# The middle heads' q of batch 0: its load goes from SyncE's queue to ScalarE's, behind an activation-table load

## The chip, the cores and the metric

The kernel runs on one core of a Trainium2 chip. The metric is the device time of one execution in microseconds (us), lower is better. Besides the unprofiled runs there is one profiled execution, from which all rows shown here come. Times inside an execution count from the start of its span.

## The reference

Eight batches of twelve heads of attention, each head 448 positions of 64 values, feed a two-layer network with a tanh GELU. All inputs and the output are float32.

```python
def rmsnorm(x, g):
    rms = np.sqrt(np.mean(x * x, axis=-1, keepdims=True) + 1e-06)
    return x / rms * g
q_n, k_n = (rmsnorm(q, g_q), rmsnorm(k, g_k))      # q, k, v: (8, 12, 448, 64)
scores = q_n @ k_n^T / sqrt(64)
attn = softmax(scores) @ v
x = attn with the heads side by side               # (3584, 768)
out = gelu_tanh(x @ w_in) @ w_out                  # w_in (768, 2048), w_out (2048, 768)
```

## The kernel before, in words

Heads are handled in groups of four. A batch `b` has three groups, `c` = 0, 1, 2, and for each group and each of q and k there is one tile, `raw`, of 128 partitions by 896 float32 (448 KB, two pairs of heads). The "middle heads" of batch 0 are the group `c` = 1. In the profile every such tile is called rawq or rawk, whatever its batch and group.

A tile goes through these steps before it can be used: it is squared (`square`, line 159 on ScalarE or line 161 on GpSimd), the squares are summed per row on VectorE (`total`, line 170), ScalarE turns the sums into reciprocal roots with a logarithm and an exponential (`rsqrt`, lines 195 to 214), and the tile is multiplied by them (`normed`, line 273). Then TensorE transposes it (`turn`, line 291) and VectorE or ScalarE copies the transposed tile out of PSUM (`put`, lines 300 to 304). `unit(b, c, t)` is one step of attention: TensorE makes a block of scores (line 333) and ScalarE takes its exponential (line 337). One batch has 21 units. After the units of batch 0 the kernel goes over to the network's matrices and the other batches, where TensorE sets the pace.

The order of instructions on each engine is the order in which the program is written (a manual schedule); nothing is moved by a scheduler. A load is a DMA that is issued by the queue of one engine: SyncE's, ScalarE's or GpSimd's. A tile's landing is told by one of eight semaphores that the DMAs of SyncE and ScalarE take in turn, so a DMA may have to wait until the one that had its semaphore before has landed.

At the start, the queues are filled so:

- SyncE's queue: the first half of q of group 0 (line 121), k of group 0 in two parts (line 617), then by `loads(0, 1)` and `loads(0, 2)` the 448 KB tiles q and k of group 1, q and k of group 2 (line 121), then the tiles of batch 1.
- ScalarE's queue: the second half of q of group 0 (line 121), the 64 values of `g_k` (line 86), then the load of the activation table of exponential and logarithm (line 627). Its next instructions are the squares of group 0, which wait for those loads.
- GpSimd's queue: the 64 values of `g_q`, and after some setting up a half of the normalization of group 0's q, then the square of group 1's q, the square of group 1's k in two halves, two loads of v, the squares of group 2, and parts of `w_in`:

```python
    normed(0, 0, "q", nc.gpsimd, t_first)
    ...
    square(0, 1, "q", nc.gpsimd)
    for a in range(2):
        square(0, 1, "k", nc.gpsimd, slice(a, a + 1))
    load_v(0, 0, 2)
```

The roots of group 1 are asked for after the third unit (`(2, lambda: rsqrt(0, 1, near=(0, 1)), ...)`), so ScalarE has three exponentials ahead of them, and all later exponentials behind them. VectorE has the sums of group 1 ahead of the copy of the second part of group 0's transposed k (`put(0, 0, "k", t_rest)`, line 300), which the fifth unit on TensorE needs.

Of the kernel before, what the change touches and what calls it, by code (L numbers as in the profile page):

```python
# [17 lines left out]
def kernel(  # L18
# [11 lines left out]
    nc = tc.nc  # L30
# [84 lines left out]
    def load(b, c, n, parts=1, engs=(nc.sync,)):  # L115
        t = rawqk.tile([P, 2, NT, D], F32, tag=f"raw{n}", name=f"raw{n}")
        src = {"q": q, "k": k}[n]
        raws[n, b, c] = t
        m = 2 // parts
        return [  # L120
            lambda i=i: engs[i].dma_start(
                t[:, i * m:(i + 1) * m].rearrange("p a t d -> p a (t d)"),
                src[b, 4 * c + 2 * i * m:4 * c + 2 * (i + 1) * m].rearrange(
                    "(a r) (p t) d -> (r p) a (t d)", r=2, t=NT
                ),
            )
            for i in range(parts)
        ]

    def loads(b, c):  # L130
        for n in "qk":
            for go in load(b, c, n):
                go()
# [491 lines left out]
        go()  # L625
    load_g(1, g_k, nc.scalar)
    nc.scalar.preload_act_table_set(EXP_SET)
    loads(0, 1)
    loads(0, 2)

    nc.vector.memset(eps, 1e-6)
# [264 lines left out]
```

## Time and profile before

| | |
|---|---|
| median of three runs | 404.31 us (404.3, 404.31, 408.4) |
| time of the profiled execution | 405.4 us |
| its span, first to last instruction | 403.6 us |
| TensorE busy with matmuls | 393.4 us, 97% of the span |
| ScalarE, VectorE, GpSimd busy | 281.0, 257.7, 123.0 us |
| mean granted TensorE clock | 0.999 of full speed |
| moved by DMA | 54.07 MB |

The engines' shares are means over the whole span. The change lies in the first 15 us, where the shares say little; what matters there is which instruction waits for which load, and that is read from the chain of work that ended last, from the waits and from the DMA issues. "SPq", "ACTq" and "POOLq" are the queues of SyncE, ScalarE and GpSimd; among the DMA queues q1 is fed by SyncE, q10 by ScalarE, q0 by GpSimd.

### The profile page before, as it was taken

What the parts mean: (1) busy time and instruction counts of PE and PEld (TensorE: products, weight loads), DVE (VectorE), ACT (ScalarE), POOL (GpSimd) and SP (SyncE); (2) the same over time, 40 slices, a digit from 0 to 9 for tenths busy, and PEclk for the clock granted to TensorE, in tenths of its full rate; (3) what the DMA queues carried; (4) which work ended last, traced back from release to release, by engine and by line L of the source; (5) the groups of instructions that cost most, each with busy time, mean ns of one, the idle gap of its engine ahead of it and who ended that gap; (6) DMA issues with size and microseconds to landing.
All of it is one profiled execution on the core that took longest, in us unless ns stands there. A gap on an engine that the chain in (4) does not pass through costs nothing.

```text
span 403.6 us, 8096 instructions
## 1 busy us (share of the span) xinstructions
PE 393.4 (97%) x3321; PEld 209.8 (52%) x3321; DVE 257.7 (64%) x436; ACT 281.0 (70%) x382; POOL 123.0 (30%) x103
## 2 busy tenths in 40 slices
PE   7799999999999999999999999999999999999996
PEld 3365555555555555554555555555555545555564
DVE  5998858985796369845699357963698405990010
ACT  6995498868974887847975689748878359744301
POOL 4993407364007230093004540072301800000000
PEclk9999999999999999999999999999999999999999
DMA  8999995998515954169612938139413511110033
GB/s 280 312 212 208 200 211 210 239 233 228 97 41 105 256 97 143 41 162 288 107 41 63 255 60 221 40 85 275 69 41 80 115 24 39 50 47 24 2 78 80
DMA packets 65561, 54.07 MB, mean 134 GB/s; under 512 B 37364, under 2 KB 60532, under 8 KB 65524
## 3 DMA queue, kind: packets, MB, share of 16 engines
q1 hardware_dynamic: 53184, 41.48, 38.3%
q0 software_dynamic: 12112, 11.80, 18.8%
q8 instruction: 26, 0.43, 0.4%
q10 hardware_dynamic: 228, 0.28, 0.3%
q14 instruction: 11, 0.09, 0.1%
HBM read 45.61 MB, written 11.01 MB: 140 GB/s over the span
## 4 chain that ended last, share of the span: by engine, by line
PE 94%; ACT 2%; DMA 2%; POOL 1%; DVE 0%; SPq 0%; issue 0%
PE o L443 38%; PE h L422 24%; PE t L473 12%; PE t L333 9%; PE t L384 8%; ACT ex L337 2%; DMA rawq<-in_q_dram 2%; PE o L384 1%; POOL g L161 1%; PE tp L291 1%; SPq L617 0%; PE os L384 0%; DVE st L393 0%; DVE ss L170 0%; PE o L266 0%
## 5 line engine op out<-in xcount | busy, mean ns | idle before, releaser
L337 ACT ACTIVATE ex<-t,shift 128x896 bf16<-128x896 f32 x168 | 157.6, 1005 | 22.0 <-PE t L333 19.4
L443 PE MATMUL o<-wout,g 128*128 128x384 bf16 (+1 forms) x912 | 156.8, 324 | 0.0
L443 PEld LDWEIGHTS <-g 128*128 128x128 bf16 x912 | 83.6, 98 | 67.7 <-issue 18.8
L422 PE MATMUL h<-xT,win 128*128 128x448 bf16 x516 | 99.1, 352 | 0.0
L170 DVE TENSOR_REDUCE ss<-sq 128x14 f32<-128x896 f32 (+3 forms) x45 | 44.3, 999 | 49.1 <-ACT sq L159 46.1
L422 PEld LDWEIGHTS <-win 128*128 128x128 bf16 x516 | 50.5, 98 | 47.1
L428 ACT ACTIVATE g<-h 128x448 bf16<-128x448 f32 x86 | 46.6, 543 | 28.2 <-PE h L422 23.1
L453 DVE COPY osb<-o 128x384 f32<-128x384 f32 x41 | 22.7, 554 | 52.6 <-PE o L443 50.6
L333 PE MATMUL t<-qT,kT 64*64 64x448 bf16 x672 | 47.0, 359 | 3.0 <-DVE kT L300 1.0
L473 PE MATMUL t<-xT,win 128*128 128x448 bf16 x252 | 49.6, 352 | 0.0
L478 ACT ACTIVATE g<-t 128x896 bf16<-128x896 f32 x21 | 18.4, 915 | 33.0 <-PE t L473 33.0
L666 POOL COPY mark<-es 1x1 bf16<-1x1 bf16 x6 | 1.1, 177 | 131.5 <-DVE es L355 131.5
L273 POOL TENSOR_TENSOR nrmq<-rawq,rinv 128x896 bf16<-128x896 f32 (+1 forms) x21 | 34.8, 1658 | 12.0 <-DVE o L236 7.7
L473 PEld LDWEIGHTS <-win 128*128 128x128 bf16 x252 | 24.5, 98 | 22.8 <-issue 0.6
L273 POOL TENSOR_TENSOR nrmk<-rawk,rinv 128x896 bf16<-128x896 f32 x20 | 33.5, 1679 | 0.0
L333 PEld LDWEIGHTS <-kT 64*64 64x64 bf16 x672 | 17.4, 105 | 28.1 <-issue 20.8
L384 PE MATMUL t<-ex,vb 64*64 64x448 bf16 x588 | 31.6, 350 | 0.0
L451 ACT COPY osb<-o 128x384 f32<-128x384 f32 (+1 forms) x16 | 7.3, 458 | 31.5 <-PE o L443 31.5
L400 DVE STREAM_TRANSPOSE rb<-rc 128x896 f32<-128x896 f32 x24 | 26.7, 1111 | 0.8
L358 DVE TENSOR_TENSOR e<-ex 128x896 bf16<-128x896 bf16 x33 | 20.0, 607 | 9.7 <-ACT ex L337 9.4
L384 PEld LDWEIGHTS <-vb 64*64 64x64 bf16 x672 | 20.4, 107 | 11.1 <-issue 2.4
L393 DVE STREAM_TRANSPOSE st<-t 128x448 f32<-128x448 f32 x42 | 24.6, 625 | 1.0 <-PE t L384 0.9
(93 smaller groups left out, 294.5 us busy)
## 6 DMA issues: line engine op xcount, KB each, us to landing
out_dram<-osb SPq DMA_DIRECT2D x54, 192.0 KB, 2.7
rawq<-in_q_dram SPq DMA_DIRECT2D x23, 448.0 KB, 4.3
rawk<-in_k_dram SPq DMA_DIRECT2D x23, 448.0 KB, 5.5
vb<-in_v_dram POOLq DMA_DIRECT2D x7, 672.0 KB, 6.7
win<-in_moe_w_in_dram POOLq DMA_DIRECT2D x8, 384.0 KB, 11.0
wout<-in_moe_w_out_dram POOLq DMA_DIRECT2D x2, 1536.0 KB, 24.0
vb<-in_v_dram POOLq DMA_DIRECT2D x1, 448.0 KB, 10.5
qT<-nrmq SPq DMA_TRANSPOSE x19, 4.9
```

Source lines behind the costliest of these rows:

```text
L170: nc.vector.reduce_sum(sss[b][:, seat(b, c), "qk".index(n), hs, ts], squares(b, c, n, hs, ts), axis=AX.X)
L273: eng.tensor_mul(nrms[n, b, c][:, ts].rearrange("p t a d -> p a t d"), raws[n, b, c][:, :, ts], root[:, :, ts].to_broadcast([P, 2, m, D]),)
L333: nc.tensor.matmul(sc[r * R:(r + 1) * R, a, :S], kT[rs, c, t, r], qT[b][rs, c, :, r], start=True, stop=True,)
L337: nc.scalar.activation(ex[:, t], sc[:, :, :S], AF.Exp, scale=scale, bias=shift)
L384: nc.tensor.matmul(o[r][a * D:(a + 1) * D], vb[b % 2][rs, 2 * c + a, i] if what else ones[rs], es[i][rs, a], start=(i == 0), stop=(i == n ...
L393: nc.vector.transpose(st[:, r].rearrange("p a b -> p (a b)"), oas[0][r])
L400: nc.vector.transpose(rb.rearrange("p r s -> p (r s)"), rc.to_broadcast([128, 2 * S // 32, 32]))
L422: nc.tensor.matmul(h[:, :S], win[:, c, f * 128:(f + 1) * 128], xT[b][:, c], start=(c == 0), stop=(c == HP - 1),)
L428: nc.scalar.activation(g[:, f, (b % 2) * S:(b % 2 + 1) * S], h[:, :S], AF.Gelu_apprx_tanh)
L443: nc.tensor.matmul(o, g[:, f, i * 128:(i + 1) * 128], wout[:, f, lo:hi], start=(f == 0), stop=(f == nf - 1),)
L453: nc.vector.tensor_copy(osb[:, lo:hi], o)
L473: nc.tensor.matmul(h[:, j, :S], win[:, c, f * 128:(f + 1) * 128], xT[b][:, c], start=(c == 0), stop=(c == HP - 1),)
```

## The change

The one load of q of group 1 of batch 0 is issued by ScalarE, behind the table load, and not by SyncE. The loads that stood behind it in SyncE's queue move up by one place. No byte more or less is loaded, no other instruction is added or taken away, and the order of the other engines stays as it was. The semaphores are dealt out a little differently: q of group 1 takes the one that k of group 1 had, and the other way round.

```diff
     load_g(1, g_k, nc.scalar)
     nc.scalar.preload_act_table_set(EXP_SET)
-    loads(0, 1)
+
+    for go in load(0, 1, "q", 1, (nc.scalar,)) + load(0, 1, "k"):
+        go()
     loads(0, 2)
```

`loads(b, c)` issued q and then k of a group, both on SyncE; `load(b, c, n, parts, engs)` gives the issues of one tile, each on the engine named.

## The prediction

> **What bounds the kernel now.** I read the page first, for the engine that sets the end. TensorE is busy for 97% of the span, and it makes up 94% of the chain that ended last. DMA has 2% of that chain, and that is what this change touches.
>
> ```profile
> span 403.6 us, 8096 instructions
> PE 393.4 (97%) x3321; PEld 209.8 (52%) x3321; DVE 257.7 (64%) x436; ACT 281.0 (70%) x382; POOL 123.0 (30%) x103
> PE 94%; ACT 2%; DMA 2%; POOL 1%; DVE 0%; SPq 0%; issue 0%
> ```
>
> Second, the chain in order of time over the first 45 us, to see where those 2% lie. Columns: start, length, what.
>
> ```profile
> 2.20 6.35 DMA rawq<-in_q_dram
> 8.55 0.07 issue
> 8.62 3.47 POOL g L161 x3
> ...
> 12.12 0.63 DVE ss L170
> ...
> 12.77 0.33 ACT lg L195
> ...
> 13.32 0.93 ACT ex L337
> ```
>
> The load of group 1's q, the one that is moved, is itself on the chain: issued at 2.20, landed at 8.55, then GpSimd's three squares of group 1, VectorE's last sum, ScalarE's roots, and from 13.3 the exponentials. So any microsecond by which this landing moves, moves the chain. ScalarE is then full: between 13.25 and the end of its table load at 31.97 its timeline shows one gap, of 0.15 us. TensorE starts the network at 31.50, and the waits after that name nothing that TensorE waits for beyond its own issue. So nothing later absorbs a shift, and a shift of the landing goes to the end one to one.
>
> Third, the timeline of the first microseconds, with the queues. Columns: start, length, engine, line, operation.
>
> ```profile
> 1.19 1.10 ACTq L86 DMA_DIRECT2D grow<-in_g_k_dram  x1
> 2.20 0.47 SPq L121 DMA_DIRECT2D rawq<-in_q_dram  x1
> 2.32 1.28 ACT L627 ACT_TABLE_LOAD   x1 [2.32 <-POOL ident masks.py:197]
> 2.71 0.47 SPq L121 DMA_DIRECT2D rawk<-in_k_dram  x1
> 4.12 1.05 ACT L159 ACTIVATE sq<-rawq 128x448 f32<-128x448 f32 x2 [0.52 <-DMA rawq<-in_q_dram]
> 8.62 1.68 POOL L161 TENSOR_TENSOR g<-rawq 128x896 f32<-128x896 f32 x1 [0.98 <-DMA rawq<-in_q_dram]
> 12.77 0.32 ACT L195 ACTIVATE lg<-ss,eps 128x28 f32<-128x28 f32 x1 [0.77 <-DVE ss L170]
> ```
>
> GpSimd sits idle for 0.98 us for the moved load, and ScalarE for 0.77 us for the roots' sums. These two are all that an earlier landing could win.
>
> **The change part by part.**
>
> *The issue.* On SyncE one issue of 0.47 us goes from 2.20, so k of group 1 is issued at 2.20 in place of 2.71 and q of group 2 at 2.71 in place of 3.23. The next one, k of group 2, stays at 3.91: it waits (0.2 us in SyncE's own waits) until the half tile on ScalarE's queue, which had its semaphore, has landed. The tiles of batch 1 behind it wait in the same way or for buffers, so they stay too. On ScalarE the issue comes after the table load in program order, and it waits for no semaphore. When does it start? The trace shows ScalarE's sequencer running past a table load: at 76.35 a table load starts in the engine, and the sequencer had finished the waits of the two squares behind that load at 76.10 and 76.19. So I take the issue right behind that of `g_k`, at 2.32 or a little later, not at 3.60. It costs 0.37 to 0.47 by the rows of 448 KB, 0.83 by the longest one (SyncE's at 4.33), 1.10 by that of `g_k`. What is queued behind it on ScalarE is the first square, which waits for its own load until 4.12. An issue that ends by 3.4 is hidden by the table load. If it started only after the table load, it would end at 4.07 (0.47, still hidden), 4.43 (0.83) or 4.70 (1.10); the last is 0.58 late for the squares of group 0, and the 0.77 us that ScalarE idles before 12.77 takes it up. The issue itself therefore costs 0.
>
> *The place among the loads.* This is the whole price. The 16 DMA engines are busy from 3 us on (a share of 0.92 to 1.06 in every microsecond), so a tile lands when the bytes ahead of it are done. The issues of the trace, taken one by one, give the landings of the 448 KB tiles on SyncE's queue, in their order: q of group 1 at 8.55 (2.20 + 6.35), k of group 1 at 9.76 (2.71 + 7.05), q of group 2 at 10.95 (3.23 + 7.72), k of group 2 at 12.15 (3.91 + 8.24): 1.2 us a tile. Each line below is the answer for one issue; the last column is the time to landing.
>
> ```profile
> rawq<-in_q_dram SPq DMA_DIRECT2D x1, 448.0 KB, 6.3
> rawk<-in_k_dram SPq DMA_DIRECT2D x1, 448.0 KB, 7.0
> rawq<-in_q_dram SPq DMA_DIRECT2D x1, 448.0 KB, 7.7
> ```
>
> After the change k of group 1 is issued first, and q 0.12 us or more behind it, on another queue. How do the DMA engines serve two queues? The row that answers is at 16.5 to 17.5: a q tile had been issued by SyncE at 14.50 and landed only 7.3 us later, and for this whole microsecond the engines moved packets of GpSimd's queue alone, whose loads of v had been issued from 12.03 on.
>
> ```profile
> q0 software_dynamic: 206, 0.18, 113.1%
> ```
>
> There is no line of q1 in that answer: the later queue waited for most of the earlier one's bytes. Where both queues were issued together (the halves of group 0's q, both at 0.74) they moved together, 24 packets of q1 and 23 of q10 between 2.6 and 2.8. And `g_k`, issued on ScalarE's queue between the two parts of group 0's k, moved at 4.0 to 4.5, amid those parts, though its queue was empty from 3.5. All three rows say: nearly in the order of issue. So q of group 1, issued almost together with k, shares its bytes with k, and both are done when both are done: at 9.76, where k lands now.
>
> The Trainium skill, page "DMA: Bandwidth & Descriptors", section "Queues, rings and completion order", says otherwise: each DMA engine goes round the queues that have work, packet by packet. By it q would have half the rate from its start on, and would land early. The microsecond without q1 does not agree with it, at least not over some 30 packets of an engine; what the sum would be is the first rival.
>
> *The sum.* Landing 9.76 in place of 8.55: +1.21. GpSimd starts the square at 9.83, k has landed by then, so its 3.47 us end at 13.30 in place of 12.09. VectorE, ScalarE's roots and the exponentials follow, each 1.21 later. On VectorE the copy of group 0's k (line 300, at 12.65) stands behind the last sum, so TensorE's fifth unit, now at 13.12, comes later by the same; TensorE's gap there grows from 0.91 to some 2.1 us. Behind GpSimd's squares stand its loads of v and `w_in`; they shift alike, and so do their users. Moved 1.21 us, nothing else: 405.4 + 1.2 = 406.6 us for a profiled execution, whose 405.4 is the span's 403.6 and 1.8 around it. The median of the runs is 1.1 us below the profiled one, so 404.3 + 1.2 = **405.5 us**.
>
> *The bounds.* From below: the landing can be earlier, but the chain wins no more than GpSimd's 0.98 of idle time, and k, the second tile needed, still lands at about 9.76, when both tiles' bytes are done: GpSimd would square its two halves (2 x 0.93) by 11.65, 0.44 earlier. From above: q falls behind q of group 2 (issued at 2.71), landing 10.95, +2.4, or behind k of group 2, 12.15, +3.6; or behind all that SyncE has queued. I take +1.2, because an issue at about 2.35 is nearest to the one at 2.20.
>
> **The rivals.**
>
> *Shared packet by packet from the start (faster).* q's first packets come 1.04 us after the issue, as those of the first half tile on ScalarE's queue did, so at 3.4, and its 16 packets an engine (256 rows of 1,792 bytes over 16 engines) alternate with those of k of group 0. At twice 74 ns, the mean of such a packet in the trace, it is done by about 6, and with the 2 us by which the slowest engines trail (the 16 landings of the tile now spread from 6.26 to 8.55) by 8. For it: the two halves at 2.6. Against it: the second at 16.5. Time: -0.44, so 403.9 us.
>
> *The issue waits for the table load.* It then starts at 3.62, after SyncE's q of group 2 and before k of group 2 (3.91): landing at 10.95, +2.4, so 406.7 us. If its issue is as long as that of `g_k` (1.10), it falls behind k of group 2 too: 12.15, +3.6, 407.9. Against it: the waits that were over before 76.35. For it: no DMA issue behind a table load is in the trace. The skill, page "ScalarE: Activation LUTs", section "What ACT_TABLE_LOAD costs", adds a drain of about 1.38 us to the 1.28 of a load, by which the issue would start at about 5.0 and the time would be estimated at 408; the trace does not agree: the load at 51.66 ends at 52.94 and the next exponential starts at 52.96.
>
> *ScalarE's queue is starved (slower).* SyncE keeps its queue full until the tiles that are issued at 4.33 and 5.20 have landed, at 13.35 and 14.56. If q gets its turn only when that stream ends, as the q tile issued at 14.50 did behind v, it lands at about 14.5: +6.0, so 410.3 us. It decides for "slower by over 1%" once the landing is past 12.6. Against it: `g_k` was served within 3 us amid the same stream.
>
> **How the numbers follow.** Chances: the forecast 0.47, packet by packet 0.27, the table load in the way 0.13, starved 0.13. A difference of 1% (4 us) is about what a measurement of this kernel can tell from no change; the three runs already spread over 4.1 us. Nothing in the profile pays 4 us, so faster by over 1% gets 0.02, slower gets the starved queue's 0.13 and 0.01 for a stall that I don't see, within 1% the other 0.84. The range runs from the packet-by-packet case (403.9) to the place behind k of group 2 (407.9), each with a few tenths for the spread of runs, 403.6 to 408.0, and leaves out the starved case.
>
> **What would show it.** ScalarE's issue row of 448 KB at about 2.35, beside the table load and not behind it; that tile's time to landing near 7.4; k's landing within 0.3 us of q's; GpSimd's square of it at about 9.8 and ScalarE's roots at about 14.0; a busy sum of TensorE as before. If the landing lies below 8.5, the order of issue is the wrong rule; if the issue lies at 3.6, the sequencer is; if roots are late by 1.2 and the end is not, the one-to-one step is.

## The result, and the profile after

The change makes the kernel a little slower. Over 22 runs of each the median is 407.23 us (405.33 to 410.44) after the change and 404.52 us (404.17 to 408.4) before it, a ratio of 1.0061 with a 95% interval from 1.0044 to 1.0077. The medians are 2.7 us apart, more than the 1.2 us of the forecast; 407.23 is inside its range, and the difference is under 1%.

The profiled execution of after took 405.71 us, only 0.3 us more than that of before. So the two profiles show about a ninth of the difference; the rest has to be found in executions that these two are not typical of. The page of after:

```profile
span 403.9 us, 8097 instructions
PE 394.5 (98%) x3321; PEld 209.9 (52%) x3321; DVE 257.7 (64%) x436; ACT 281.2 (70%) x382; POOL 123.0 (30%) x103
PE 94%; ACT 2%; DMA 2%; POOL 1%; DVE 0%; issue 0%; POOLq 0%; ACTq 0%
```

Nothing moved between the engines, and TensorE still has 94% of the chain. The chain of waits of after over the first microseconds (start, length, what) has the same members as before:

```profile
2.36 6.51 DMA rawq<-in_q_dram
8.86 0.07 issue
8.93 1.89 POOL g L161 x2
...
12.42 0.63 DVE ss L170
13.08 0.33 ACT lg L195
13.62 0.93 ACT ex L337
```

The moved load is still the one that starts the chain. It lands at 8.86 instead of 8.55, and ScalarE's logarithm (line 195), the first step of the roots, starts at 13.08 instead of 12.77: both 0.31 us later, as the span is 0.3 us longer. The timeline of after (start, length, engine, line, operation, and in brackets the idle time before it and what ended it):

```profile
2.17 0.47 SPq L121 DMA_DIRECT2D rawk<-in_k_dram  x1
2.32 1.28 ACT L627 ACT_TABLE_LOAD   x1 [2.32 <-POOL ident masks.py:197]
2.36 0.39 ACTq L121 DMA_DIRECT2D rawq<-in_q_dram  x1
2.69 0.47 SPq L121 DMA_DIRECT2D rawq<-in_q_dram  x1
8.93 1.68 POOL L161 TENSOR_TENSOR g<-rawq 128x896 f32<-128x896 f32 x1 [1.41 <-DMA rawq<-in_q_dram]
13.42 0.38 PE L333 MATMUL t<-qT,kT 64*64 64x448 bf16 x4 [1.34 <-ACT lg L195]
```

ScalarE issues the load at 2.36, 0.04 us after its table load has begun and 0.19 us behind SyncE's issue of k. GpSimd idles 1.41 us for the tile (0.98 before), and TensorE's gap ahead of the fifth unit is 1.34 us (0.91 before).

### The profile page after: what moved, and what is told of

It reads as the page before. It is cut to its first block, busy times and chain, and to the rows that moved or that the text cites. A ratio compares the mean times of both kernels' runs of the same rounds, so it can differ in the third digit from the quotient of the medians.

```text
span 403.9 us, 8097 instructions
## 1 busy us (share of the span) xinstructions
PE 394.5 (98%) x3321; PEld 209.9 (52%) x3321; DVE 257.7 (64%) x436; ACT 281.2 (70%) x382; POOL 123.0 (30%) x103
## 4 chain that ended last, share of the span: by engine, by line
PE 94%; ACT 2%; DMA 2%; POOL 1%; DVE 0%; issue 0%; POOLq 0%; ACTq 0%
PE o L443 38%; PE h L422 24%; PE t L473 12%; PE t L333 9%; PE t L384 8%; DMA rawq<-in_q_dram 2%; ACT ex L337 2%; PE o L384 1%; PE tp L291 1%; POOL g L161 1%; PE os L384 0%; POOL grow L86 0%; DVE st L393 0%; DVE ss L170 0%; PE o L266 0%
```

## The experiments

Two theories were set against each other. Theory A: ScalarE's queue is beside the point; what counts is that q of group 1 is now issued behind k of group 1, which moves the whole chain by a place, and that the longer gap of TensorE can bring its clock down. Theory B: something of ScalarE's queue is irregular, by which the load sometimes lands very late.

### The changed kernel again

> The changed kernel once more, for a second profiled execution and more times. Theory A (place and clock): q of group 1 lands 1.2 to 2 us later than in a usual execution of before, and where TensorE's gap ahead of the fifth unit is long the granted clock falls below 1.0 for a while and costs another 1 to 3 us; then the runs with a mean clock of 0.99 are the long ones and the median is again near 407. Theory B (the queue): ScalarE's queue is served irregularly, the landing scatters by some us, and the clock has no part; then long and short runs have the same clock.

It took 408.06 us (405.3 to 409.46, 12 runs) against 404.53 us (35 runs of before), ratio 1.0065 (1.0038 to 1.0091). This profile fell into a long execution: 408.39 us, span 406.6. The load landed at 9.08 and the logarithm started at 13.29, only 0.21 us later than in the first profile of after, and yet the span is 2.7 us longer. Where it went is seen in the windows of this execution (stretch, its length and busy us of TensorE, weight loads, VectorE, ScalarE, GpSimd, the granted clock, DMA share, GB/s):

```profile
11.00:14.50 3.50, 2.18 (x18) 0.59 (x15) 3.04 (x5) 2.29 (x5) 3.50 (x5) 1.00 1.06 381
14.50:18.00 3.50, 2.80 (x23) 1.61 (x22) 2.50 (x5) 3.07 (x4) 3.50 (x3) 0.56 1.21 211
18.00:21.50 3.50, 3.31 (x36) 1.62 (x40) 2.44 (x4) 2.19 (x3) 1.91 (x4) 0.50 1.07 304
21.50:25.00 3.50, 2.99 (x51) 1.31 (x43) 3.17 (x6) 2.95 (x6) 3.03 (x2) 0.97 1.11 208
```

The column of the clock reads 0.56, 0.50, 0.97: behind the gap of 1.32 us ahead of the fifth unit TensorE runs at half its clock, from 14.90 to 21.73, which is 6.83 us. In the same two stretches it does 23 and 36 matmuls where the third experiment below, at full clock, does 42 and 54. Theory A's second half is seen here; theory B's very late landing is not.

### The order alone, on SyncE's queue

```diff
-    loads(0, 1)
+    for go in load(0, 1, "k") + load(0, 1, "q"):
+        go()
     loads(0, 2)
```

> Both loads of group 1 stay on SyncE's queue, but k is issued ahead of q; ScalarE issues nothing more than before. Theory A: what counts is that q is done with or behind k, so the time is that of the changed kernel within 0.5 us, 406.5 to 407.5, with q landing 1.2 us behind k. Theory B: without ScalarE's queue the loss is at most q's one place in the order, 1.2 us, so 405.7 or less, and the scatter is that of before.

It took 407.64 us (405.04 to 409.23), ratio 1.0052 (1.0024 to 1.008). The timeline of this kernel:

```profile
2.18 0.47 SPq L121 DMA_DIRECT2D rawk<-in_k_dram  x1
2.69 0.99 SPq L121 DMA_DIRECT2D rawq<-in_q_dram  x2
9.09 1.68 POOL L161 TENSOR_TENSOR g<-rawq 128x896 f32<-128x896 f32 x1 [1.70 <-DMA rawq<-in_q_dram]
```

With both loads in SyncE's queue and nothing on ScalarE's, q lands at 9.02, the logarithm starts at 13.24, the clock drops as before (half from 14.74 to 21.57), and the time is that of the change: 1.0052 against 1.0065, with intervals that overlap. The median is 0.1 us above what theory A expected. So theory B falls: as far as 12 runs can tell, which is to some 0.3%, the change is a change of order, made by way of another queue. One thing differs: here k lands at 7.7 (2.18 + 5.5), 1.3 us ahead of q, while in the changed kernel it lands together with q.

### After, with the gap filled

The kernel has dummy matmuls, `idle(n, ...)`, whose results nobody reads. This kernel puts seven of them in place of two ahead of the fifth unit; it is otherwise the changed one.

```diff
-            lambda: normed(0, 1, "k", nc.vector, t_rest), lambda: idle(2, warm())),
+            lambda: normed(0, 1, "k", nc.vector, t_rest), lambda: idle(7, warm())),
```

> The changed kernel with seven instead of two idle matmuls ahead of the fifth unit, some 1.4 us more work for TensorE in the gap in which it waits for group 0's transposed k. Theory A: the clock stays at 1.0, and the time falls by what the clock had cost, to 405.5 to 406.2. Theory B: the idle matmuls end before TensorE is needed, so the time stays at 407.2, or is some tenths longer where they end late.

It took 406.64 us (405.78 to 409.59), ratio 1.0052 (1.0026 to 1.0079): 0.4 us above the upper end of what was expected, since 3 of the 12 runs still had a lower clock. The other 9, at full clock, have a median of 406.07, which lies inside. Its profiled execution is the twin that the long one needs: the logarithm starts at 13.24, the gap ahead of the fifth unit is 0.63 us, and the clock stays up. The windows of this kernel, the same stretches:

```profile
11.00:14.50 3.50, 2.83 (x19) 1.05 (x18) 3.05 (x5) 2.03 (x4) 3.50 (x5) 1.00 1.06 384
14.50:18.00 3.50, 2.64 (x42) 1.69 (x45) 3.42 (x7) 3.35 (x5) 3.50 (x4) 1.00 1.24 218
18.00:21.50 3.50, 2.72 (x54) 1.38 (x50) 3.50 (x7) 3.47 (x7) 3.19 (x4) 1.00 1.08 313
```

Its span is 404.08 us; that of the second experiment, with the logarithm at the same 13.24, is 406.56. The difference, 2.5 us, is the price of half the clock for 6.83 us. That the filling keeps the clock up more often is read from the counts, 3 of 12 runs at a lower clock against 21 of 34 of the changed kernel; the medians alone, 406.64 and 407.23, would not tell the two kernels apart.

### Before, with the same filling

> The kernel before with the same seven idle matmuls, as a control. Theory A: the gap of before is short (0.9 us), the clock is already at 1.0 in most runs, so 404.3 to 405.0: the idle matmuls outlast the gap by some tenths, and win only in the few long runs. Theory B: 404.5, with the same few long runs.

The same edit on the kernel before: 404.78 us (404.51 to 405.9), ratio 0.9986 (0.9962 to 1.0011), all 12 runs at full clock. The ratio hides a small price, since three of the 35 runs beside it are long ones at a lower clock: against the 404.5 of the others the seven idle matmuls cost some 0.3 us, as their expectation allowed. The 406.07 of the third experiment is 1.3 us above 404.78; the two kernels differ in the moved load alone, so that is the price of the later landing.

### Before, with a larger gap and no load touched

```diff
-           (2, lambda: rsqrt(0, 1, near=(0, 1)), lambda: idle(2, warm())),
+           (2, lambda: rsqrt(0, 1, near=(0, 1))),
...
-            lambda: normed(0, 1, "k", nc.vector, t_rest), lambda: idle(2, warm())),
+            lambda: normed(0, 1, "k", nc.vector, t_rest)),
```

> The kernel before without the two pairs of idle matmuls that follow the third and the fourth unit; no load is touched. It tells the clock from the landing. Theory A: the landing of q stays where it was (8.5 or earlier), TensorE's gap grows by some 0.5 us, and the granted clock falls to half for 6.8 us in half of the runs or more, which are 2 to 3.5 us longer: a median of 405.5 to 407.5. Theory B (the clock has no part, or only follows the landing): 404.5, with no more long runs than before.

It took 405.29 us (404.28 to 408.23) against 404.51 (35 runs), ratio 1.0006 (0.9974 to 1.0038). The median hides two groups: 7 runs at full clock with a median of 404.41, and 5 at a lower one with 406.98. The median is 0.2 us below what theory A expected, and 5 of 12 is less than its half. Beside 5 of the 35 runs of before at a lower clock that is a weak difference; beside the 9 of 88 counted below it is a clearer one. No load was moved, so the gap by itself seems to bring the clock down, in some executions, at a price of 2.6 us. None of these five was profiled: the profile of this kernel, with a gap of 1.73 us, is at full clock.

### One place further back

```diff
-    loads(0, 1)
-    loads(0, 2)
+    for go in load(0, 1, "k") + load(0, 2, "q") + load(0, 1, "q") + load(0, 2, "k"):
+        go()
```

> On SyncE's queue q of group 1 is issued behind k of group 1 and q of group 2, so by two places later than in the kernel before. Theory A: a place is worth 1.2 us, so q lands 2.4 us later than before, TensorE's gap is over 2.5 us in every execution and the clock falls in nearly all of them: 404.5 + 2.4 + 2.5 = 409.4 (408.5 to 410.5). If places cost nothing and the clock alone counts: no more than in the changed kernel, 407 to 408.

It took 408.57 us (406.2 to 410.01), ratio 1.0078 (1.005 to 1.0105), inside what was expected. The load landed at 10.06, and the gap was 2.66 us, as the bracket of this row of the kernel's timeline says:

```profile
14.62 0.59 PE L333 MATMUL t<-qT,kT 64*64 64x448 bf16 x4 [2.66 <-ACT lg L195]
```

Eleven of 12 runs had a lower clock, against 21 of 34 of the changed kernel and 9 of 88 of before: the larger the gap, the oftener.

### One place further forward

Here q of group 1 is issued by ScalarE ahead of `g_k`, so that it is the earliest of the 448 KB tiles.

```diff
+    load_q1 = load(0, 1, "q", 1, (nc.scalar,))
+    load_q1[0]()
     load_g(1, g_k, nc.scalar)
...
-    loads(0, 1)
+    for go in load(0, 1, "k"):
+        go()
```

> ScalarE issues q of group 1, but ahead of g_k and of the table load, at about 1.2; k of group 1 stays with SyncE and moves up as in the changed kernel. Theory A: q then lands before k, at 7 to 8, GpSimd squares it right after its half of group 0's q, and the chain wins up to 0.8 us, with no run at a lower clock: 403.7 to 404.4. Theory B (ScalarE's queue is the trouble): as the changed kernel, 407.

This missed: 406.59 us (405.06 to 408.13), ratio 1.0026 (0.9996 to 1.0056). The load itself did what the order says, issued at 1.20 and landed at 6.30. But loads of group 0 came late. The timeline of this kernel:

```profile
5.45 0.63 ACT L159 ACTIVATE sq<-rawk 128x512 f32<-128x512 f32 x1 [0.30 <-DMA rawk<-in_k_dram]
6.57 0.56 POOL L678 TENSOR_TENSOR gprod<-grow 64x32 f32<-64x32 f32 x2 [3.94 <-DMA grow<-in_g_q_dram]
7.89 0.19 PE L707 MATMUL t<-gbf,rows 32*128 32x32 bf16 x2 [1.57 <-DVE nrmq L273]
8.42 1.67 POOL L161 TENSOR_TENSOR g<-rawq 128x896 f32<-128x896 f32 x1
```

The last row has no bracket: GpSimd doesn't wait for this tile any more. It came late itself, because the 64 values that it multiplies at 6.57 landed late: its wait is 3.94 us, and 4.13 in the next experiment, against 2.29 to 2.81 in the twelve profiles where q is not first. That q's bytes went ahead of them is the likely reason; no run tests it alone. TensorE's first gap, 1.57 us, now ends at 7.89. The gap itself is not new. The first profile of before has a longer one, which ends at 7.18, and its clock stays up:

```profile
7.18 0.19 PE L704 MATMUL t<-gbf,rows 32*128 32x32 bf16 x2 [1.88 <-DVE nrmq L273]
```

So the length of a gap alone does not decide about the clock; where it lies counts too, as is shown further down. Ten of 12 runs had a lower clock (median 406.7); the two others, with a median of 405.29, give no sign that anything is won at full clock.

> The kernel with q first on ScalarE's queue, and four instead of two idle matmuls ahead of the fifth unit. Theory A: with the early landing the gap is short and the clock is safe already, so the same as without them or some tenths longer, 403.8 to 404.6; any gain would lie in the few runs at a lower clock.

The same with four idle matmuls ahead of the fifth unit took 406.52 us (405.22 to 407.92), ratio 1.0025 (0.9996 to 1.0055), and missed as well. In its profile the clock drops at 8.20, behind the early gap (2.28 us there) and ahead of the added matmuls, so these came too late.

### Executions of before, and one more of after

The first two profiles gave a step of 0.31 us for the landing, the forecast 1.21, the runs more. Since the landing differs from one execution to the next, three more executions were profiled.

> The kernel before, unchanged, for another profiled execution. The first one took 405.4 us, 0.9 above the median of the timed runs, with q of group 1 landing at 8.55 and two landings trailing the others by 1.2 us. If that tail is what the usual execution lacks (theory A), an execution of 404.5 or less shows q landing at 7.5 or earlier and GpSimd's square right behind its part of group 0's q. If every profiled execution has the tail, this one is at 405.4 to 406 again, and the landing of the usual execution stays unseen.

> The kernel before, unchanged, once more, for the same reason: at 404.5 or less with an early landing of q, or at 405.4 to 406 with a late one.

> The changed kernel once more, for a third profiled execution. At the full clock the span is the time of the second logarithm of the roots plus 390.85 us (7 executions so far); theory A: this holds again, with that logarithm at 13.0 to 14, so a span of 403.9 to 404.9; and 2.5 us more if the clock was at half for 6.8 us.

The three took 405.03, 404.65 and 406.23 us, all at full clock; the two of before lie between the times that were expected, and the one of after, with a span of 404.45, is as expected. In the first, GpSimd does not wait for the tile at all (it landed at 8.1): the first part of group 0's k had landed only at 5.8 and set the pace, so the moved load does not start the chain in every execution. The second (before) and the third (after) lie near the medians of full-clock runs, 404.51 and 406.19. The timeline of that execution of before, and under it that of after:

```profile
7.86 1.68 POOL L161 TENSOR_TENSOR g<-rawq 128x896 f32<-128x896 f32 x1 [0.40 <-DMA rawq<-in_q_dram]
12.01 0.32 ACT L195 ACTIVATE lg<-ss,eps 128x28 f32<-128x28 f32 x1 [0.19 <-DVE ss L170]
12.36 0.38 PE L333 MATMUL t<-qT,kT 64*64 64x448 bf16 x4 [0.33 <-ACT lg L195]
```

```profile
9.43 1.68 POOL L161 TENSOR_TENSOR g<-rawq 128x896 f32<-128x896 f32 x1 [1.98 <-DMA rawq<-in_q_dram]
13.58 0.32 ACT L195 ACTIVATE lg<-ss,eps 128x28 f32<-128x28 f32 x1 [1.77 <-DVE ss L170]
13.93 0.38 PE L333 MATMUL t<-qT,kT 64*64 64x448 bf16 x4 [1.91 <-ACT lg L195]
```

The landings are 7.79 and 9.37, 1.58 us apart; squares and logarithm are 1.57 apart, and the spans, 402.87 and 404.45, 1.58 apart. TensorE's gap goes from 0.33 to 1.91 us. The execution of before on which the forecast was made had its load land at 8.55, 0.76 us later than this one, so it left less to lose.

The two were picked for their times, and the last landings alone would say less: they are 7.79 to 9.03 in the six profiles with q ahead of k (before and its variants with idle matmuls) and 8.86 to 9.37 in the four of the changed kernel with and without filling, 0.6 us apart in the mean. The trace has 16 landings for each of these tiles, and it is the last that counts. Their median is steadier: 6.3 to 6.8 in the six, 8.0 to 8.2 in the four, so the tile as a whole comes some 1.6 us later, and what scatters is its last one to four landings.

### Two more idle matmuls in the kernel before

> The kernel before with four instead of two idle matmuls ahead of the fifth unit: enough to fill a gap of 0.9 us, where seven outlast it. Theory A: the runs at a lower clock (9 of 70 so far in the kernel before) go, and those at the full clock stay where they are: a median of 404.4 to 404.6, with none above 406.5. If the idle matmuls cost time themselves: 404.8 as with seven.

It took 405.11 us (404.26 to 406.51) against 404.89 (17 runs), ratio 1.0001 (0.9984 to 1.0019), and so missed the 404.4 to 404.6 that was expected. One of its 12 runs had a lower clock, and one of the 17 beside it; that is no gain. No version here beats the kernel before.

## Why the prediction was right, and where it fell short

**The issue costs nothing: right.** The row of 448 KB stands on ScalarE's queue at 2.36 beside the table load, as the forecast had it (2.35), and ScalarE's first square of group 0 starts at 4.01, not later than before. The rival in which the issue waits for the table load is out.

**Order of issue decides the place: right for the landing, not for every packet.** q shares the engines with k instead of coming ahead of it: 8.86 behind k's 8.09 in the first profile of after, 9.37 beside k's 9.16 in the last. The forecast's sign, k within 0.3 us of q, held in the second (0.21) and not in the first (0.77). The packet-by-packet rival (a landing by 8, 403.9 us) and the starved one (14.5, 410.3 us) are out. The packets of the first profile of after show how. ScalarE's queue issued the tile at 2.36 and moved hardly a packet of it before 4.5, when the first packets of k's tile moved too; until then group 0's k was served. From 5.5 to 7.0 it moved 143 packets beside 175 of SyncE's queue. The rule of the Trainium skill, page "DMA: Bandwidth & Descriptors", section "Queues, rings and completion order", by which the engines go round the queues packet by packet, agrees with these near-equal shares, but not with the two microseconds before them. So the packet-by-packet rival was wrong in its start, not in its sharing. The experiment with the order alone shows what the second queue did: q's landing is the same without it, as far as one profile and 12 runs can tell, and k's is earlier.

**One to one to the end: shown, at full clock.** In nine profiled executions of six kernels at full clock, from a logarithm at 12.01 to one at 13.58, the span minus the start of that logarithm is 390.85 us, within 0.03. Nothing behind the roots absorbs any of it.

**The step of +1.21 us: too small.** It was the difference between two landings in one execution, 8.55 and 9.76. The two executions near the medians landed at 7.79 and 9.37, so the term is about +1.58; the medians of full-clock runs give +1.68 (406.19 of 13 runs less 404.51 of 79). One doubt is left: all six profiles with q ahead of k are of executions longer than 404.51, so no landing of an execution as short as the median was seen. GpSimd's square came at 8.93 to 9.43 and the roots at 13.08 to 13.58, not at the predicted 9.8 and 14.0: the forecast's landing was too late, but the starting point that it was set against was later still.

**TensorE's gap had no price: the term that was missed.** The forecast said that the gap grows to some 2.1 us (it is 1.3 to 1.9) and put nothing beside it. Its price is the clock. Of the 34 runs of the changed kernel 21 have a mean granted clock under 0.998 of full speed, with a median of 408.27 us, 2.1 above that of its full-clock runs. Of 88 runs of before, taken beside the experiments, 9 do, with 408.3; that is 3.8 above its full-clock runs, more than the 2.5 of the clock, so these may have landed late as well, but none was profiled. Put together, place and clock make the means of all runs 407.58 and 405.18 us, 2.4 apart: 1.6 is the difference of the full-clock means (406.44 and 404.83), the place, and the other 0.8 is a clock that drops in 62% of executions instead of 10%.

**The range held partly by luck.** It was drawn from places in the queue, with no term for the clock, and a clock that falls in most executions still landed in it. The rival in which the issue waits for the table load, at 406.7 to 407.9, is even nearer to the median than the forecast; only the row at 2.36 shows that its mechanism is not what happened.

**Why one execution drops and another does not.** The clock's stretches are multiples of 3.41 us (10.24 or 3.41 at full clock, counted from where the first matmuls go from 0.58 to 0.35 us each, then 6.83 or 3.41 at half), so it seems to be decided once in 3.41 us. In the five profiles with a drop, the stretch of 3.41 us that ends where the clock falls has little matmul work in it. Two of them, first the changed kernel run again, then the kernel with q one place further forward (columns as above):

```profile
11.49:14.90 3.41, 1.78 (x17) 0.60 (x16) 2.95 (x6) 2.20 (x5) 3.41 (x5) 1.00 1.07 370
```

```profile
5.57:8.98 3.41, 1.68 (x18) 0.93 (x16) 2.70 (x6) 2.43 (x9) 2.26 (x5) 1.00 1.04 383
```

The other three have 1.50, 1.15 and 0.98 us. In the executions without a drop the stretches can be counted on from where the clock came up (to about 0.1 us). In the first profile of after they cut the gap, which lies at 12.08 to 13.42, at 12.51:

```profile
9.09:12.51 3.42, 3.00 (x23) 0.85 (x21) 2.23 (x5) 2.79 (x3) 3.42 (x4) 1.00 1.06 386
12.51:15.92 3.41, 2.17 (x23) 1.15 (x24) 3.12 (x6) 2.81 (x5) 3.41 (x4) 1.00 1.14 305
```

Each part keeps 2.17 us or more, and the clock stays. The gap is as long as that of the long execution (1.34 and 1.32 us); only the cut differs. In all nine full-clock profiles the emptiest of the first stretches after the clock came up holds 1.84 us or more (1.84, give or take 0.1, in the first of before, then 1.88, 1.89 and from 2.03 up). So the border lies near 1.8 us of matmuls in 3.41, about half; 1.78 and 1.84 are closer to each other than the stretches can be placed. This is read from the profiles; no run set the phase itself. The Trainium skill, page "TensorE: Matmul & The Clock Gate", section "The HAM clock gate (the "warmup" mystery)", gives the window as free-running and 3413 ns long, which the stretches agree with. The same section of the Trainium skill lets the clock fall after an idle window of some 3.4 us; here the traces differ, since a window with 1.78 us of matmuls in it was enough.

**What stays open.** Two runs of the changed kernel took 408.24 and 408.94 us at a mean clock of 0.999 and 0.998; a run of before took 409.21 at 1.000. None of the profiles caught such a one. And why a load that SyncE issues at 2.2 lands anywhere from 7.79 to 9.03, with one to four of its 16 landings trailing, was not tried.

## What to carry to other kernels

A load at the start of the chain is priced by its place in the order of issue over all queues: another engine's queue brought no earlier landing, and when it was brought forward, loads that had been ahead of it came later. Where start-up loads scatter, one profile gives one draw; profile several executions of the kernel before making a difference out of two landings, and compare the bulk of a tile's landings as well as the last. And a gap of TensorE that an edit lengthens past a microsecond, as here, wants a price of its own, the clock, beside the wait itself.

## What the runs showed of the hardware

- A gap of TensorE of 1.3 us was enough to halve its clock for 6.83 us, when the 3.41 us around it held 1.78 us of matmuls; it cost 2.5 us, more than the shift that made the gap. A gap of 1.88 us elsewhere left the clock up.
- Two queues with a tile each got near-equal shares of the packets, 143 and 175 in 1.5 us. But a tile on a queue with little left ahead of it began no earlier than the other queue's tile, which was issued at 2.17 behind the larger part of the loads: issued at 2.36, it had moved hardly a packet by 4.5.
- A half clock for one such stretch (3.41 us) cost 0.9 us: the kernel with q one place further back had its logarithm at 14.27 and a span of 405.99, 0.87 over 14.27 + 390.85.
- A DMA issue on ScalarE's queue starts 0.04 us after a table load that stands ahead of it in the program has begun (2.32 and 2.36), so a table load doesn't hold it up.
